# The last quarter of Q by seven-product runs, reciprocals stored on the ACT queue, and a later second weight block

## The chip, the cores and the metric

The kernel runs on one core of one Trainium2 chip. The metric is the device time of one execution in microseconds; smaller is better. The program has five instruction streams that meet only at semaphores: PE (TensorE), DVE (VectorE), ACT (ScalarE), POOL (GpSimd) and SP (SyncE, which here only issues transfers).

## The reference

One transformer block on 2048 tokens (S) of width 1024 (D): a linear attention with 32 heads of 32, and then an MLP that mixes the tokens.

```
x = A_x;  phi = lambda t: where(t > 0, t + 1, exp(t)) + 1e-6
q, k, v = split(layernorm(x) @ wqkv)            # 1024 x 3072
kv  = einsum("bhsd,bhse->bhde", phi(k), v);  z = sum_s phi(k)
num = einsum("bhqd,bhde->bhqe", phi(q), kv)
den = einsum("bhqd,bhd->bhq", phi(q), z)[..., None] + 1e-6
h   = x + (num / den) @ wo
out = h + (gelu(layernorm(h)^T @ w1 + b1) @ w2 + b2)^T    # w1: 2048 x 3584
```

## The kernel before

The work is done in four stages, one after the other.

**Projection stage.** x is normalized and transposed (`xnT`). K and V are made for pairs of token blocks q = 1 to 7 by "runs": a run computes a product of 2 x 2 blocks with seven multiplications instead of eight (Winograd's scheme), p1 to p7, each of four 512-column matmuls. The sums of blocks that it needs are made by DVE (`x_sums`, `w_sums`). `run_step` (L1117) lays two runs over each other: it starts run n and finishes run `prev`, and puts each copy and sum between the matmuls by hand.

Q is kept transposed as `pqT`, eight blocks j of 128 rows for each quarter u of the tokens (512 tokens each), after phi. There are two ways to make it. `q_unit` (and `q_held`, the same with its place in the order fixed) makes one block (u, j) by eight 512-column matmuls; its phi takes an exp and a relu on ACT and two operations on DVE. `QRun` (L1084) makes half a quarter (four j) by the seven products, each of eight 256-column matmuls; before, this is used for quarter u = 2 alone, with two runs laid among the K and V runs of q = 5. The other quarters, u = 0, 1 and 3, are plain units, listed in `q_units` (L1308): eight of them (u = 0) fill places in the projection stage, sixteen (u = 1 and u = 3) come after it.

`kv_accum(i)` adds token block i to kv and z in three PSUM banks; after the last block DVE moves them to `kvbd` and `zz`.

**Fold loop** (L1571). Each turn n makes one remaining Q unit with `q_held`. In turns 1 to 8 it also calls `fold(n - 1)`, two matmuls that multiply kv into wo; ACT copies one result out and DVE the other. PSUM tiles come from a ring of five (`acc_tile`). For each quarter the loop further does:

- `den(u)`: eight matmuls of phi(q) with z (`den_mm`), then on ACT a Ln and an Exp that leave the reciprocal in the one buffer `rd_sb`, and a transfer of it to DRAM (`den_inv`);
- `den_spread(u)`: eight transfers that read it back, repeated over 32 partitions each, into two of three SBUF buffers (`thirds`);
- `scale_q(u, h)`: one DVE multiplication of half a quarter of `pqT`, 128 x 2048 elements.

`den_at`, `spread_at` and `scale_at` give the turns in which they stand. `first_sums` makes sums of the first block of w1 on DVE in the turns of `sums_at`: four `asums` (128 x 2048 each) and four small ones.

**Output stage** (L1598). For each of 16 token blocks i, `seed` lets ACT copy x into two PSUM tiles, `out_mm` adds 16 matmuls of `pqT` with the folded wo, and `out_evac` copies the result to h (ACT) and takes its statistics (DVE). `normalize_h` and `combine_h` prepare the MLP's operand on DVE. Block i reads quarter i // 4 of `pqT`; within one tile the first four matmuls read the half h = 0 and the last four h = 1.

**MLP stages.** Two stages of nested seven-product schemes follow. They are the longer half of the time and the change does not touch their code.

Nearly all instructions of the fold loop and the output stage go through wrappers (`hv`, `ht`, `hs`, `hd` for DVE, PE, ACT and SP) that keep the written order, so that an engine does its instructions strictly as the Python code lists them; they all show line L234, that of the wrapper. Transfers go out on SP's queue in the written order too, and one that waits holds up all behind it.

## Time and profile before

| what | value |
|---|---|
| median of 5 runs | 559.14 us (558.59 to 559.59) |
| the profiled execution: its own time | 559.14 us |
| its span in the profile | 557.3 us |
| granted TensorE clock | 1.0 |
| projection stage, until the last `kv_accum` ends | to 137.4 us |
| fold loop, with the transposes of kv | 142.6 to 176.9 us |
| output stage | 176.9 to 232.8 us |
| PE, DVE, ACT busy, of the span | 99%, 80%, 52% |

A busy PE in this profile only says that matmuls were in flight. What tells whether PE loses time is the distance from the start of one group of matmuls to the start of the next, and whether the next group starts late.

### The profile page before, as it was taken

Reading aid. Unit: us, or ns where it says so; the run is one execution under the profiler, and the core shown is the slowest. Engines: PE = TensorE matmul, PEld = TensorE weight load, DVE = VectorE, ACT = ScalarE, POOL = GpSimd, SP = SyncE. Lnnn points to the kernel's source line nnn. Section 1 sums busy time; section 2 is a strip of 40 time slices with the busy share of each in tenths; the row PEclk is TensorE's granted clock in tenths of the full one; section 3 lists DMA queues with packets and bytes.
Section 4 is the critical chain, followed back from the end, with each engine's and each line's share of the span. In section 5 each row is a group of like instructions: output and inputs, shape, how many; then the busy total and the mean of one; then the engine's idle time right before and its main releaser. Section 6 shows DMA issues by size and latency. Waiting matters only on the chain.

```text
span 557.3 us, 8932 instructions
## 1 busy us (share of the span) xinstructions
PE 551.7 (99%) x3387; PEld 320.4 (57%) x3387; DVE 443.9 (80%) x858; ACT 288.9 (52%) x614; POOL 26.2 (5%) x36
## 2 busy tenths in 40 slices
PE   8999999999999999999999999999999999999997
PEld 3444446645444444456666766666444667667665
DVE  6898888764488688889989789887996879749747
ACT  5747678665776877646556465464210412413311
POOL 1000000000000000000000000000003103103111
PEclk9999999999999999999999999999999999999999
DMA  8933341202966961102140440413769649849434
GB/s 299 306 76 76 84 88 20 39 0 76 313 159 183 331 187 75 76 0 94 60 152 7 145 138 16 151 42 92 204 204 237 195 131 247 208 130 233 94 106 75
DMA packets 83931, 74.51 MB, mean 134 GB/s; under 512 B 15650, under 2 KB 76336, under 8 KB 83888
## 3 DMA queue, kind: packets, MB, share of 16 engines
q1 hardware_dynamic: 79504, 69.87, 42.2%
q0 software_dynamic: 4096, 3.68, 5.1%
q8 instruction: 26, 0.43, 0.3%
q10 hardware_dynamic: 288, 0.39, 0.2%
q14 instruction: 17, 0.14, 0.1%
HBM read 59.12 MB, written 11.67 MB: 127 GB/s over the span
## 4 chain that ended last, share of the span: by engine, by line
PE 92%; DMA 3%; DVE 2%; ACT 1%; issue 0%; ACTq 0%; DVEq 0%
PE psI L234 23%; PE psC L234 14%; PE acc_t L234 14%; PE psB L234 8%; PE psC L966 4%; PE psB L966 4%; PE psA L966 4%; PE acc_t L888 3%; PE acc_t L1298 2%; PE psB L346 2%; PE psA L346 2%; PE psE L966 2%; PE psC L346 2%; DMA wq<-in_B_w_dram 2%; PE kvps L917 1%; PE psA L234 1%
## 5 line engine op out<-in xcount | busy, mean ns | idle before, releaser
L234 PEld LDWEIGHTS <-is 128*128 128x128 f16 x736 | 71.8, 98 | 31.4 <-DVE is L234 0.5
L234 PEld LDWEIGHTS <-sa 128*128 128x128 f16 x606 | 59.2, 98 | 27.5 <-issue 0.4
L234 PEld LDWEIGHTS <-wq 128*128 128x128 bf16 (+1 forms) x496 | 48.5, 98 | 28.2 <-issue 1.2
L234 PE MATMUL acc_t<-wo_sb,pqT 128*128 128x512 f16 x256 | 55.6, 379 | 0.0
L491 POOL DMA_DIRECT2D out_dram<-wq x28 | 24.3, 927 | 519.3 <-ACT wq L494 487.3
L234 PEld LDWEIGHTS <-pqT 128*128 128x128 bf16 x256 | 25.0, 98 | 30.5 <-issue 0.6
L234 DVE TENSOR_TENSOR t<-psI,t 128x256 f32<-128x256 f32 (+1 forms) x45 | 20.8, 475 | 22.2 <-PE psI L234 20.9
L194 DVE TENSOR_SCALAR e_sb<-e_sb 128x512 bf16<-128x512 bf16 x64 | 18.4, 288 | 21.7 <-ACT e_sb L189 21.5
L234 PE MATMUL psC<-gs,wq 128*128 128x512 f16 x140 | 34.1, 379 | 0.0
L966 PEld LDWEIGHTS <-xs 128*128 128x128 f16 x208 | 20.1, 98 | 22.1 <-DVE xs L955 0.6
L234 PE MATMUL psC<-hT,sa 128*128 128x512 f16 x112 | 31.2, 379 | 0.0
L234 PE MATMUL psI<-hi,is 128*128 128x256 f16 x200 | 30.0, 273 | 0.0
L234 PE MATMUL psB<-hT,sa 128*128 128x512 f16 x112 | 29.7, 379 | 0.0
L234 PE MATMUL acc_t<-xnT,wq_sb 128*128 128x512 bf16 x128 | 29.4, 379 | 0.1
L189 ACT ACTIVATE e_sb<-acc_t 128x512 bf16<-128x512 f32 x32 | 19.1, 598 | 18.6 <-PE acc_t L1298 10.0
L234 DVE BATCH_NORM_STATS2 hst<-acc_t 128x6 f32<-128x512 f32 x32 | 21.4, 692 | 9.1 <-ACT h_bf L234 8.9
L966 PE MATMUL psA<-wkv,xnT 128*128 128x512 bf16 x104 | 26.7, 379 | 0.0
L966 PEld LDWEIGHTS <-xnT 128*128 128x128 bf16 x156 | 15.2, 98 | 18.1 <-issue 0.2
L234 PE MATMUL psC<-hT,wq 128*128 128x512 f16 x96 | 24.6, 379 | 0.0
L234 ACT CAST h_bf<-acc_t 128x512 bf16<-128x512 f32 x32 | 18.4, 582 | 12.0 <-PE acc_t L234 12.0
L234 DVE TENSOR_TENSOR e<-psI,es 128x256 f32<-128x256 f32 x20 | 8.5, 425 | 19.9 <-PE psI L234 19.9
L234 ACT COPY psI<-psI 128x256 f32<-128x256 f32 x50 | 18.0, 360 | 11.6 <-PE psI L234 9.7
(246 smaller groups left out, 1132.7 us busy)
## 6 DMA issues: line engine op xcount, KB each, us to landing
wq<-in_B_w_dram SPq DMA_DIRECT2D x14, 1024.0 KB, 8.0
wq<-in_B_w_dram SPq DMA_DIRECT2D x12, 896.0 KB, 7.4
gs<-parked SPq DMA_DIRECT2D x9, 896.0 KB, 4.7
shared_sb<-rd_dram SPq DMA_DIRECT2D x32, 128.0 KB, 3.8
out_dram<-h_bf SPq DMA_DIRECT2D x16, 256.0 KB, 2.0
x_sb<-in_A_x_dram SPq DMA_DIRECT2D x14, 256.0 KB, 3.0
w2o<-in_B_w_dram SPq DMA_DIRECT2D x4, 896.0 KB, 11.0
out_dram<-wq POOLq DMA_DIRECT2D x28, 128.0 KB, 4.6
```

The source lines that it names most:

```text
L189: pin(nc.scalar.activation(e_sb[:], src, ACT.Exp))
L194: pin(nc.vector.tensor_scalar(e_sb[:], e_sb[:], 1.0, PHI_EPS, ALU.min, ALU.add))
L234: return (lambda *a, **kw: pin(op(*a, **kw))) if self.always or getattr(Held, self.key) else op
L346: pe.matmul(ps[:, cols], lhsT=lhs[:, k, :], rhs=mv(k)[:, cols], start=(start and k == 0), stop=(k == self.nk - 1), skip_group_check=True,)
L491: nc.gpsimd.dma_start(to, ot[:, a:b], accum_op=ALU.add)
L888: mm = nc.tensor.matmul(pp[:, 0:CW], lhsT=xnT[:, kt, i * P:(i + 1) * P], rhs=wkv[:, kt, c * CW:(c + 1) * CW], start=(kt == 0), stop=(kt == ...
L917: pin(nc.tensor.matmul(kv_ps[b][:, sl, :], lhsT=pks[i % NPK][:, j * P:(j + 1) * P], rhs=vaugs[i % NVA][:, j, :], start=False, stop=(i == N ...
L966: pin(nc.tensor.matmul(ps[:], lhsT=lhs[:, k, :], rhs=rhs[:, k, :], start=(start and k == 0), stop=(k == hk2 - 1), skip_group_check=True,))
L1298: nc.tensor.matmul(qp[:, 0:SW], lhsT=wq_sb[:, kt, j * P:(j + 1) * P], rhs=xnT[:, kt, u * SW:(u + 1) * SW], start=(kt == 0), stop=(kt == ND ...
```

## The change

Quarter u = 3 is made by two `QRun`s as well. They come after the K and V runs of q = 7, and the last two `kv_accum` move into the second of them. The operands that the Q runs borrow from `pqT` (`later`) lie in other places of it. Of the plain units thirteen are left where there were twenty-one: one beside the end of the last run, and twelve in the fold loop (u = 0, blocks 4 to 7, and u = 1).

In the fold loop the order of the quarters changes: the reciprocals come in the order 2, 0, 3, and 1, whose heads are done in two halves, the second one in the output stage, between the two tiles of block 0. For the halves the unused rows of `zz` are set to S by two small memsets in turn 7. The store of each reciprocal goes out on ACT's queue instead of SP's. The first weight block and the x blocks are loaded later (turns 0 and 6), the second weight block at blocks 8 and 9 of the output stage instead of turns 12 and 13. One `asums` moves to block 10 of the output stage, as does one `scale_q` to block 0 and one to block 2. `TURN` rotates the ring of PSUM tiles once.

```diff
--- before.py
+++ after.py
@@ -819,7 +819,7 @@
                 t.bitcast(FP16).rearrange("p (k c) -> p k c", c=CW)
                 for t in (wo_sb[:, 2 * t:2 * t + 2, :].rearrange("p a b -> p (a b)") for t in range(4))
             ]
-            later = [pqT[:, j:j + 4, u * SW:(u + 1) * SW].bitcast(FP16) for u, j in ((1, 0), (NSC - 1, 0), (NSC - 1, 4))]
+            later = [pqT[:, j:j + 4, u * SW:(u + 1) * SW].bitcast(FP16) for u, j in ((1, 0), (1, 4), (0, 4))]
             tk = [t.bitcast(FP16).rearrange("p (k c) -> p k c", c=CW) for t in thirds] + [later[0]]
             tq = [
                 t.bitcast(FP16).rearrange("p (k j f) -> p k j f", k=ND // 2, f=P)
@@ -1305,7 +1305,7 @@
                 phi_evac(pqT[:, j, u * SW:(u + 1) * SW], qp[:, 0:SW], SW, a2k)
 
             assert NSC == 4
-            q_units = [(u, j) for u in (0, 1, NSC - 1) for j in range(ND)]
+            q_units = [(u, j) for u in range(2) for j in range(ND)]
             NVP = NS // 2
             q_next = iter(q_units)
 
@@ -1338,6 +1338,8 @@
                 runs = [KRun(q), VRun(q)]
                 if q == 5:
                     runs = [runs[0], QRun(q // 2, 0), runs[1], QRun(q // 2, 1)]
+                elif q == NVP - 1:
+                    runs += [QRun(q // 2, 0), QRun(q // 2, 1)]
                 for n in runs:
                     kind = type(n).__name__[0]
                     i = {"K": 2 * q + 3, "V": 2 * q + 4}.get(kind, NS)
@@ -1354,6 +1356,9 @@
                         if kind == "V":
                             kv_accum(2 * q - 2)
                             kv_accum(2 * q - 1)
+                        if kind == "Q" and q == NVP - 1 and n.half == 1:
+                            kv_accum(NS - 2)
+                            kv_accum(NS - 1)
                         if i < NS:
                             ln_finish(i)
                             load_next(i + 2)
@@ -1361,7 +1366,7 @@
                     def after7():
                         if kind == "V" and q != 5 and q + 1 < NVP:
                             x_sums(q + 1)
-                        if kind == "Q" and n.half == 1:
+                        if kind == "Q" and n.half == 1 and q + 1 < NVP:
                             x_sums(q + 1, slice(0, 3))
                         if kind == "K" and q in q_sums:
                             w_sums(qmov, q_sums[q])
@@ -1373,11 +1378,7 @@
                     run_step(n, prev, after6, after5, after7, after3=after3)
                     prev = n
             run_step(None, prev, fill=q_fill)
-            q_fill()
-            kv_accum(NS - 2)
-            kv_accum(NS - 1)
-            for n in range(3):
-                q_fill()
+            q_left = list(q_next)
             nc.vector.memset(zz[:, :, 0:3 * HB], 0.0)
             nc.vector.memset(zz[:, :, 3 * HB:], float(S))
             for b in range(NKB):
@@ -1408,6 +1409,7 @@
         pools["is_bufs"] = 4
         a3p = actx.enter_context(ExitStack())
         ndp = a3p.enter_context(tc.tile_pool(name="ndp", bufs=3, space=PSUM))
+        rd_half = dram.tile([P, SW], FP16, name="rd_half")
         rd_dram = [dram.tile([P, SW], FP16, name=f"rd_dram{u}") for u in range(NSC)]
 
         with ExitStack() as a3:
@@ -1428,33 +1430,34 @@
                     (hs.copy if c == 0 else hv.tensor_copy)(wf[:, j, cols], ps[:, 0:CW])
 
             rdbs = {}
-            SPREAD = (0, 2, 1, 3)
+            SPREAD = (2, 0, 1, 3)
+            TURN = 9
             NH = ND // 2
 
-            def den_mm(u):
+            def den_mm(u, os=(0, 1)):
                 ps = ndp.tile([P, SW], F32, tag="den", name="den_ps")
-                for o in range(2):
+                for o in os:
                     for g in range(4):
                         j = 4 * o + g
                         ht.matmul(
                             ps[g * QR:(g + 1) * QR, :],
                             lhsT=zz[:, j, (1 - o) * HB:(1 - o) * HB + QR],
                             rhs=pqT[:, j, u * SW:(u + 1) * SW],
-                            start=(o == 0),
-                            stop=(o == 1),
+                            start=(o == os[0]),
+                            stop=(o == os[-1]),
                             skip_group_check=True,
                             tile_position=(0, g * QR),
                         )
                 return ps
 
-            def den_inv(u, ps):
+            def den_inv(ps, to):
                 hs.activation(ps[:], ps[:], ACT.Ln, bias=eps_den[:], scale=1.0 / S)
                 hs.activation(rd_sb, ps[:], ACT.Exp, scale=-1.0)
-                hd.dma_start(rd_dram[u][:], rd_sb)
-
-            def den_spread(u):
-                rows = rd_dram[u].rearrange("(g o h) n -> o h g n", g=4, h=HB)
-                for h in range(2):
+                hs.dma_start(to[:], rd_sb)
+
+            def den_spread(u, halves=(0, 1)):
+                for h in halves:
+                    rows = (rd_half if (u, h) == (1, 0) else rd_dram[u]).rearrange("(g o h) n -> o h g n", g=4, h=HB)
                     rdb = thirds[(2 * SPREAD.index(u) + h) % 3].bitcast(FP16).rearrange("p (j n) -> p j n", n=SW)
                     for q in range(HB):
                         hd.dma_start(
@@ -1463,8 +1466,8 @@
                         )
                     rdbs[u, h] = rdb
 
-            def den(u):
-                den_inv(u, den_mm(u))
+            def den(u, os=(0, 1)):
+                den_inv(den_mm(u, os), rd_half if os == (0,) else rd_dram[u])
 
             def scale_q(u, h):
                 v = pqT[:, h * NH:(h + 1) * NH, u * SW:(u + 1) * SW]
@@ -1504,11 +1507,11 @@
 
             def place(i):
                 u, r = divmod(i, NSC)
-                return i if u != 2 else NSC * u + r % 2 * 2 + r // 2
-
-            def out_mm(i):
+                return i if u < 2 else NSC * u + r % 2 * 2 + r // 2
+
+            def out_mm(i, dcs=range(NDC)):
                 at = place(i) * P
-                for dc in range(NDC):
+                for dc in dcs:
                     for j in range(ND):
                         ht.matmul(
                             seeds[i][dc][:, 0:CW],
@@ -1546,44 +1549,52 @@
 
             for c in range(NDC):
                 load_wo(c)
-            for half in range(2):
-                load_w1(0, half, pin)
-            for i in range(XRL + 1):
-                load_xr(i)
-
             def first_sums():
                 cur = Quad([Mixer1(0), Mixer1(1)])
-                for m in (5, 6, 7, 3):
+                for m in (5, 6, 7):
                     yield pin(cur.asums(m))
                 cur.in5 = Inner(cur.sts, 5, None, "i5", cur.sink5, cur.sum5)
                 Held.on = True
                 cur.in5.sums()
                 Held.on = False
                 yield cur
+                pin(cur.asums(3))
+                yield
 
             for _ in range(2):
                 acc_ring.append(acc_ring.pop(0))
-            sums_at, ahead = (4, 8, 9, 11, 13), first_sums()
-            scale_at = {5: (0, 0), 6: (0, 1), 10: (2, 0), 12: (2, 1), 15: (1, 0)}
-            den_at = {0: 0, 2: 2, 9: 1}
-            spread_at = {0: 0, 6: 2, 12: 1}
-            kv_transpose()
-            for n, (u, j) in enumerate(q_units[8:]):
-                if n == len(q_units) - 8 - 1:
+            sums_at, ahead = (4, 5, 8, 11), first_sums()
+            scale_at = {6: (2, 0), 7: (2, 1), 9: (0, 0), 10: (0, 1)}
+            den_at = {1: 2, 4: 0, 6: NSC - 1, 8: 1}
+            spread_at = {3: 2, 6: 0, 10: 1}
+            for n, (u, j) in enumerate(q_left):
+                if n == len(q_left) - 1:
                     seed(0)
                 q_held(u, j)
+                if n == 0:
+                    kv_transpose()
+                    for half in range(2):
+                        load_w1(0, half, pin)
+                    load_xr(0)
                 if 1 <= n < 1 + ND:
                     fold(n - 1)
+                if n == 7:
+                    for at in (0, 2 * HB):
+                        hv.memset(zz[:, :, at:at + HB], float(S))
                 if n in den_at:
-                    den(den_at[n])
-                if n in spread_at:
-                    den_spread(spread_at[n])
-                if n in (12, 13):
-                    load_w1(1, n % 2, pin)
+                    den(den_at[n], (0,) if den_at[n] == 1 else (0, 1))
                 if n in scale_at:
                     scale_q(*scale_at[n])
+                if n in spread_at:
+                    den_spread(spread_at[n], (0,) if spread_at[n] == 1 else (0, 1))
+                    if n == 6:
+                        for i in range(1, XRL + 1):
+                            load_xr(i)
                 if n in sums_at:
                     cur = next(ahead)
+                if n == TURN:
+                    for _ in range(4):
+                        acc_ring.append(acc_ring.pop(0))
             xctx.close()
             a3w = a3.enter_context(tc.tile_pool(name="a3w", bufs=4))
             xr2pool = a3.enter_context(tc.tile_pool(name="xr2pool", bufs=XR2))
@@ -1594,17 +1605,26 @@
             hT2 = hpool.tile([P, NSP, CW], FP16, name="hT2")
             hT3 = hpool.tile([P, NSP, CW], FP16, name="hT3")
             hT4 = hpool.tile([P, NSP, CW], FP16, name="hT4")
-            scale_at = {0: (1, 1), 6: (3, 0), 8: (3, 1)}
+            scale_at = {0: (1, 0), 2: (1, 1), 6: (3, 0), 8: (3, 1)}
             for i in range(NS):
                 seed(i + 1)
-                out_mm(i)
                 if i == 0:
                     load_xr(XRL + 1)
-                    den(NSC - 1)
-                    for k in range(XRL + 2, XRL + XR2 + 1):
+                    out_mm(0, (0,))
+                    den(1, (1,))
+                    load_xr(XRL + 2)
+                    den_spread(1, (1,))
+                    out_mm(0, (1,))
+                    for k in range(XRL + 3, XRL + XR2 + 1):
                         load_xr(k)
-                if i == 2:
+                else:
+                    out_mm(i)
+                if i == 4:
                     den_spread(NSC - 1)
+                if i in (8, 9):
+                    load_w1(1, i % 2, pin)
+                if i == 10:
+                    next(ahead)
                 if i < NS - XRL - XR2 - 1:
                     load_xr(i + XRL + XR2 + 1)
                 if i == NS - 1:
```

## The prediction

> **What bounds the kernel now.** I read the page's engine lines first, then busy time by stretch, then the order of time on PE, DVE, ACT and SP around the fold loop.
>
> ```profile
> PE 551.7 (99%) x3387; PEld 320.4 (57%) x3387; DVE 443.9 (80%) x858; ACT 288.9 (52%) x614; POOL 26.2 (5%) x36
> ```
>
> A stretch's numbers are its length, then PE, PEld, DVE, ACT and POOL busy (instructions), the clock, the DMA share and GB/s:
>
> ```profile
> 143.00:157.00 14.00, 13.60 (x76) 5.54 (x74) 6.26 (x16) 11.23 (x21) 0.00 (x0) 1.00 0.77 253
> 157.00:177.00 20.00, 20.00 (x99) 8.78 (x98) 19.02 (x36) 14.58 (x28) 0.00 (x0) 1.00 0.61 146
> 176.88:232.79 55.91, 55.91 (x266) 25.08 (x265) 45.35 (x94) 40.59 (x96) 0.00 (x0) 1.00 0.57 186
> ```
>
> PE sets the time everywhere, at a clock of 1.00. But in the second half of the fold loop (157 to 177) DVE is busy 19.02 of 20.00 us: it works just behind PE.
>
> ```profile
> 102.58 1.04 PE L1103 MATMUL psA<-xnT,wq_sb 128*128 128x256 bf16 x8
> 103.45 1.04 PE L1103 MATMUL psE<-xs,shared_sb 128*128 128x256 f16 x8
> 131.28 1.89 PE L1298 MATMUL acc_t<-xnT,wq_sb 128*128 128x512 bf16 x8
> 133.00 1.03 PE L966 MATMUL psB<-wkv,xs 128*128 128x512 bf16 x4
> 154.26 0.38 PE L234 MATMUL acc_t<-wo_sb,kvT 128*128 128x512 bf16 x1
> 154.94 0.38 PE L234 MATMUL acc_t<-wo_sb,kvT 128*128 128x512 bf16 x1 [0.30 <-ACT r_sb L191]
> 155.42 1.89 PE L234 MATMUL acc_t<-xnT,wq_sb 128*128 128x512 bf16 x8
> ```
>
> Starts count here. A plain unit takes 1.727 us (24 matmuls in 5.18), a 256-column product 0.874 (three in 2.62), a 512-column matmul 0.216. From 154.26 to 155.42 two matmuls take 1.16 us instead of 0.43: PE lost 0.72. ACT tells why:
>
> ```profile
> 153.31 0.60 ACT L234 ACTIVATE shared_sb<-den_ps 128x512 f16<-128x512 f32 x1 [1.69 <-DMA rd_dram<-shared_sb]
> ```
>
> and the chain of waits, which shows that store:
>
> ```profile
> 147.25 5.98 DMA rd_dram<-shared_sb
> ```
>
> The Exp of the second reciprocal waited for the one buffer's first store, 5.98 us long, and all ACT copies of PSUM waited behind it. Last, DVE's spacing in the loop:
>
> ```profile
> 169.06 0.29 DVE L194 TENSOR_SCALAR e_sb<-e_sb 128x512 bf16<-128x512 bf16 x1
> 169.47 0.42 DVE L198 TENSOR_TENSOR pqT<-e_sb,r_sb 128x512 bf16<-128x512 bf16 x1
> 169.81 1.22 DVE L234 TENSOR_TENSOR pqT<-pqT,shared_sb 128x2048 bf16<-128x2048 bf16 x1
> 170.95 0.29 DVE L194 TENSOR_SCALAR e_sb<-e_sb 128x512 bf16<-128x512 bf16 x1
> ```
>
> From start to start: phi's two operations 0.39 + 0.34 = 0.73, a scaling 1.14 (an `asums` the same), and by the rows at 165.46 and 166.06 a fold copy 0.60.
>
> **The change, part by part.** The profiled execution took 559.14 us, which is also the median of the runs (its span is 557.3, the 1.8 around it are not touched); the sum is made against it.
>
> *Quarter 3 by runs.* Eight units less, 8 x 1.727 = 13.82 us; fourteen products more, 14 x 0.874 = 12.23. All of it is PE's path: -1.58. Their seven products bring per run three copies on ACT and two additions on DVE, in 6.1 us of PE; the Q runs among K and V at 86 to 112 carried more than that with no late start. The last `kv_accum` would end at 143.6; DVE then needs about 3.3 us for `kvbd`, `zz` and a run's addition, until 147, and the transposes are due at 149.66, after turn 0 (147.93 to 149.66). Covered. If it were not, each us late would cost one.
>
> By the Trainium skill (TensorE: Matmul & The Clock Gate, Back-to-back issue gap) a sustained stream has 81 ns per matmul at 128 columns and 131 at 512; a straight line between gives my estimate of 98 ns at 256, so the exchange would lose 112 x 98 - 64 x 131 = 2.6 us. The rows above show 216 and 109 ns here, and I go by them.
>
> *The stall at 154.26.* New stores are three turns, then two apart. The first is issued at 155.2 and the next Exp is due at 161.5: 6.3 us, over the 5.98. The weight block, which now waits until the last run's DVE work is done (151.0), is mostly through by then. -0.72. If the store took longer, ACT and all evacuations behind it would wait again; 1.69 us of that cost PE 0.72. What is late next is below.
>
> *Store on ACT's queue.* An issue takes 0.41 us of ACT by the row at 0.74 us (`x_sb`, ACTq), against 0.34 on SP. Per folding turn ACT works 1.46 of 2.16 us (exp 0.50, relu 0.48, copy 0.48), and a reciprocal adds 1.4 + 0.41: the lag is made up in the next turns. Nothing on the path by itself. Its landing lies, by the rows, between 1.7 us (one in light traffic) and 5.98; I take 2 to 4. By the Trainium skill (DMA: Bandwidth & Descriptors, Issuing engines are not separate DMA queues) the transfers of all queues interleave on the same 16 engines, so the other queue would not help the store against a weight block; by it the store keeps its 5.98 and the sum stays as it is.
>
> *Halving quarter 1's heads.* The same eight matmuls in two groups; a group begins 0.09 late (starts at 144.76 due, 144.85 seen): +0.09. The second Ln, Exp and store are ACT time in the output stage, where ACT is busy 40.59 of 55.91.
>
> *kv to fold.* Between the transposes and the first fold there is now one unit instead of two units and the heads. ACT needs 2.2 us from the end of a unit to the end of `kvT` (142.58 to 144.77), PE gets there 2.18 after it and needs about 0.1 more to restart: +0.15, bounds 0 and 0.5.
>
> *DVE in the shorter loop.* This decides. Turns end on PE (no stalls after the first fold) at 161.92 (n = 5), 164.08, 166.88, 169.04, 171.56, 173.29 and 175.02 (n = 11). Turn 5's phi starts its addition on DVE at 163.63, because ACT first does quarter 0's Ln, Exp and store. From there DVE has, in its fixed order: the addition, copy and `asums` (2.07), turn 6 with a scaling (2.47), turn 7 with a scaling, a short wait and the two memsets of about 0.08 each (2.69), turn 8 with `asums` (2.46), turns 9 and 10 with a scaling each (1.87 + 1.87). 13.43 in all: the last scaling, half 1 of quarter 0, ends at 177.06. `out_mm(0)` starts at 175.12 and its fifth matmul, at 175.98, reads that half: it starts at about 177.2. +1.22. The first half heads on the way wait for the memsets (end 169.72, due 169.5), a stall of 0.3 that lies within the 1.22. Before, quarter 0 was scaled eight turns before its use. Bounds: 0.4, if DVE starts its chain at turn 5's relu without the Ln and Exp before it (about 0.8 earlier); 2.0, if the weight block (issued 151.0; such loads took 5.4 to 11.0 to land) holds the first `asums`, due at 161.4, by 0.8.
>
> *Reads and x blocks.* On SP everything is queued in order: quarter 2's eight reads (from about 158), quarter 0's (the second half only after the scaling that frees its buffer at 168.2 and quarter 3's store, about 169.4), x blocks 1 to 3, then quarter 1's first half, two x blocks, its second half, six x blocks. Eight reads take about 3.6 us to issue and 3.9 to land. Quarter 0's would land at about 174.7, needed at 175.9; quarter 1's second half is stored at 180.4, read from 182.6, landed at about 188, and DVE comes to it at 188.7; PE needs it scaled at 191.4, so 190.2 would do. Covered by 1 to 2 us. x blocks come at least two blocks early.
>
> *Moved to the output stage.* One more scaling, four small sums and an `asums`: 3.7 us more DVE work on 45.35 of 55.91, spread to blocks 0, 2 and 10, where DVE idles about 1.15 per pair of blocks; it has caught up before block 15. The second weight block is issued at about 208, lands by 219 (11.0 at most), and its first use was at 246.9. Nothing.
>
> Sum: -1.58 - 0.72 + 0.09 + 0.15 + 1.22 = -0.84; 559.14 becomes 558.3. Nothing after the output stage changes its order, so the gain is carried to the end.
>
> **The rivals.** *DVE's cover holds.* If the chain on DVE ends a us earlier, only PE's terms remain: -1.58 - 0.72 + 0.09 + 0.15 = -2.06, 557.1. For it: the old loop ran 20 us at 95% DVE without a late matmul. Against it: there the last scaling before the output stage was not read at once.
>
> *A round trip of reciprocals comes late* (the slower side). In the old output stage the eight reads of quarter 3 took longer:
>
> ```profile
> 189.01 5.17 SPq L234 DMA_DIRECT2D shared_sb<-rd_dram  x8
> ```
>
> 5.17 us to issue, and with 5.0 to land (median of that stretch) about 10 us from first issue to last landing. If quarter 1's second half takes 10 us from 182.6, it lands at 192.6 instead of by 190.2. Block 4 waits 2.4 us: -0.84 + 2.4 = +1.6, 560.7. It decides from a landing at 190.2 on. Against it: then x blocks and a weight block filled the engines; now the x blocks are queued behind the reads, and there are four reads, not eight.
>
> **How the numbers follow.** A measurement of this kernel can tell about 0.2%, 1.1 us, from no change: the lines are 558.0 and 560.3. The forecast gets 0.50, with a range of its own from 557.3 to 559.4 (the stall from 0.4 to 2.0 and the `kvT` term from 0 to 0.5); 0.18 of it lies under 558.0. DVE's cover holds: 0.28. A late round trip: 0.22, of which 0.18 lies above 560.3. So faster 0.28 + 0.18 = 0.46, slower 0.18, the same 0.36. The range goes from 557.0 to 560.2; it leaves out most of the late round trip and a little below.
>
> **What would show it.** In the changed profile: fourteen more products at 0.874; no ACT wait of over a us on `rd_dram`; the first fold about 0.15 late; the first half heads waiting for a memset; and the fifth matmul of `out_mm(0)` about a us after the fourth, released by DVE's scaling. If `out_mm(0)` runs its sixteen matmuls in 3.5 us, the DVE chain was mis-sized. If block 4 starts late or DVE waits for a transfer in the output stage, the rival on the slower side holds. Wrong altogether: a late start in the projection stage after 131, or a change in the MLP stages.

## The result, and the profile after

The changed kernel takes 560.84 us (median of 33 runs, 558.72 to 563.14) where the kernel before took 559.09 in the same session (57 runs, 557.97 to 560.13). The ratio is 1.0027, with a 95% interval from 1.002 to 1.0035. A gain of 0.8 us was forecast, a loss of 1.75 came, and the new kernel's times are spread twice as wide. Its profiled execution took 561.92 us (span 560.1), one of its slower ones, so its rows show more than the median loss.

From its page, the engines and the chain that ended last (the chain by engine was PE 92%, DMA 3%, DVE 2% before):

```profile
PE 550.3 (98%) x3435; PEld 324.9 (58%) x3435; DVE 447.4 (80%) x864; ACT 291.4 (52%) x618; POOL 26.3 (5%) x36
...
PE 84%; DMA 8%; DVE 5%; ACT 2%; issue 1%; SPq 0%; ACTq 0%; DVEq 0%
```

PE was busy 1.4 us less and finished 2.8 us later: the matmuls saved are real, and transfers (8% of the chain) took the place of matmuls. Busy time by stretch (length, then PE, PEld, DVE, ACT, POOL, clock, DMA share, GB/s) says where; these are the second half of the fold loop and the output stage.

```profile
157.00:175.45 18.45, 18.24 (x98) 7.47 (x96) 15.79 (x30) 15.59 (x30) 0.00 (x0) 1.00 0.66 200
175.45:233.14 57.69, 56.02 (x261) 24.97 (x260) 48.37 (x98) 40.80 (x96) 0.00 (x0) 1.00 0.67 210
```

The output stage was 55.91 us of unbroken PE; now it is 57.69 with 56.02 busy. The starts on PE show each place (a number in brackets is the idle time before the row, and what ended it):

```profile
131.35 1.04 PE L1103 MATMUL psA<-xnT,wq_sb 128*128 128x256 bf16 x8
...
169.83 0.40 PE L234 MATMUL den_ps<-pqT,zz 128*32 128x512 bf16 x4 [0.21 <-DVE zz L234]
...
175.45 1.02 PE L234 MATMUL acc_t<-wo_sb,pqT 128*128 128x512 f16 x4
177.50 1.04 PE L234 MATMUL acc_t<-wo_sb,pqT 128*128 128x512 f16 x4 [1.03 <-DVE pqT L234]
...
198.61 34.69 PE L234 MATMUL acc_t<-wo_sb,pqT 128*128 128x512 f16 x160 [0.65 <-ACT acc_t L234]
...
474.32 0.94 PE L234 MATMUL psI<-gi,is 128*128 128x256 f16 x7 [0.94 <-DVE is L234]
```

Up to the output stage nearly all is as forecast: `out_mm(0)` starts at 175.45 instead of 176.88 (175.12 was forecast), and its fifth matmul waits for DVE. The waits at 198.61 and 474.32 were not forecast. The first is a wait for ACT, which waits for a store, and behind that stands the order of SP's queue:

```profile
196.58 1.07 ACT L234 CAST h_bf<-acc_t 128x512 bf16<-128x512 f32 x2 [3.47 <-DMA out_dram<-h_bf]
```

```profile
160.71 11.84 SPq L234 DMA_DIRECT2D shared_sb<-rd_dram  x16
172.59 3.71 SPq L234 DMA_DIRECT2D shared_sb<-in_A_x_dram  x3
...
183.96 1.75 SPq L234 DMA_DIRECT2D shared_sb<-rd_dram  x4
185.75 2.81 SPq L234 DMA_DIRECT2D xr<-in_A_x_dram  x6
...
189.73 0.34 SPq L234 DMA_DIRECT2D out_dram<-h_bf  x1
```

h has four buffers (`h_bf`). Block 0's h was ready by 181.7, but its store stands on SP behind the reads of quarter 1's second half, which wait until 183.96 for the landing of that half's reciprocals, and behind seven x blocks; it leaves at 189.73, lands at 196.50 and only then frees its buffer for block 4. Before, it left earlier, landed at 192.46, and nothing waited:

```profile
187.02 0.34 SPq L234 DMA_DIRECT2D out_dram<-h_bf  x1
```

The wait at 474.32 is DVE's, for a weight block of the second MLP stage:

```profile
472.98 0.62 DVE L234 TENSOR_TENSOR is<-wq 128x896 f16<-128x896 bf16 x1 [1.46 <-DMA wq<-in_B_w_dram]
```

Before, this operation began without a wait:

```profile
471.10 0.61 DVE L234 TENSOR_TENSOR is<-wq 128x896 f16<-128x896 bf16 x1
```

The `load_w2` calls stand at the same place against PE in both kernels (4.5 us ahead of the same matmul), yet the second block of the pair took 10.3 us to land instead of 8.0. The same happens once more at the next pair, with a wait of 0.91 us on PE at 515.33. At the end the kernel is 2.78 us behind: 0.07 from before 131, 0.28 from there to the end of the output stage, 2.43 from the MLP stages.

### The profile page after: what moved, and what is told of

The parts are those of the page before. It is cut to its first block, busy times and chain, and to the rows that moved or that the text cites. A ratio compares the mean times of both kernels' runs of the same rounds, so it can differ in the third digit from the quotient of the medians.

```text
span 560.1 us, 9040 instructions
## 1 busy us (share of the span) xinstructions
PE 550.3 (98%) x3435; PEld 324.9 (58%) x3435; DVE 447.4 (80%) x864; ACT 291.4 (52%) x618; POOL 26.3 (5%) x36
## 4 chain that ended last, share of the span: by engine, by line
PE 84%; DMA 8%; DVE 5%; ACT 2%; issue 1%; SPq 0%; ACTq 0%; DVEq 0%
PE psI L234 21%; PE psC L234 13%; PE acc_t L234 8%; PE psB L234 8%; PE psC L966 4%; PE psB L966 4%; PE psA L966 4%; DMA wq<-in_B_w_dram 4%; PE acc_t L888 3%; PE psB L346 2%; PE psA L346 2%; PE psE L966 2%; PE psC L346 2%; DVE is L234 1%; DMA shared_sb<-rd_dram 1%; PE kvps L917 1%
## 5 line engine op out<-in xcount | busy, mean ns | idle before, releaser
L234 PE MATMUL psI<-gi,is 128*128 128x256 f16 x168 | 22.3, 273 | 1.8 <-DVE is L234 1.8
L234 PE MATMUL acc_t<-xnT,wq_sb 128*128 128x512 bf16 x96 | 22.4, 379 | 0.0
## 6 DMA issues: line engine op xcount, KB each, us to landing
w2o<-in_B_w_dram SPq DMA_DIRECT2D x4, 896.0 KB, 10.3
```

The costliest lines, as they stand in the source:

```text
L234: return (lambda *a, **kw: pin(op(*a, **kw))) if self.always or getattr(Held, self.key) else op
```

## The experiments

The stages of every profiled execution, cut at starts on PE (second last pair of `kv_accum`, first matmul of `out_mm(0)`, first of each MLP stage, last matmul; the first MLP stage is 159.64 to 159.68 in all and left out). The last two columns are the first and second pair of w2 loads of the second MLP stage: when the load's last packet starts, counted from the load's issue, and in brackets when a packet of the instruction queue q8 starts amid them, less than 10 us after the issue. Times in us; the last is the profiled execution's own.

```
                                to kv   loop  output  MLP 2   w2, first     w2, second     own
before                         129.47  47.41  55.90  161.40   9.92         11.11 (8.79)  559.14
after                          129.55  45.90  57.70  163.85  12.05 (0.90)  12.06         561.92
e1 after, shared tile          129.40  46.52  58.19  163.41  13.17 (0.81)  10.00         562.37
e2 before, DRAM shifted        129.86  47.31  55.90  162.26  10.39         12.01 (9.13)  560.31
e3 before, half w2             130.54  47.35  55.90  160.86   6.88          6.62 (8.88)  559.64
e4 after, half w2              130.81  46.06  58.43  160.86   8.07 (5.73)   6.66         561.00
e5 after, x loads later        129.95  46.06  56.83  160.86   9.94 (1.02)  10.15         558.53
e6 + half rows first           130.84  46.10  57.67  162.99  12.77 (0.72)  10.32         562.46
e7 after, stores on SP         129.69  47.10  57.38  162.17  11.25 (1.58)  11.23         561.18
e8 before, stores on ACT       129.83  47.56  56.00  160.96  10.11         10.69 (8.79)  559.30
e9 before, 48 more on PE       131.18  46.98  55.90  161.78  11.51 (0.59)  10.17         560.77
e10 after, 34 more on PE       130.22  45.83  58.67  160.86   9.72         10.40         560.41
e11 e6, 34 more on PE          130.91  45.84  58.51  160.86   9.86         10.33         560.95
e12 e5, other block order      130.63  46.04  56.72  161.83  11.54 (0.65)  10.25         560.06
e13 e12, 18 more on PE         129.92  45.86  56.76  160.91  10.12         10.64         558.29
e14 after, 18 more on PE       130.54  45.86  57.35  160.86   9.99          9.98         559.46
e15 e8 again                   129.93  47.80  57.11  161.45   9.81         11.17 (9.39)  561.25
e16 e13, quarter 0 later       130.40  45.85  55.83  160.86   9.96         10.36         557.86
e17 e16, stores on POOL        131.13  45.62  55.83  162.65  10.39         12.45         560.44
e18 after, stores on POOL      129.34  45.63  57.93  160.86  10.51 (0.71)   9.94         558.93
```

The first column varies by 1.8 us whatever the kernel, so a single execution's own time settles little; the stages settle more. Each ratio below is against the kernel before on the same chip.

**Where do the late weights come from? The place in DRAM (e1, e2).** The change adds a DRAM tile, `rd_half`, which moves the parked tiles of the MLP.

```diff
 e1 (after)
-        rd_half = dram.tile([P, SW], FP16, name="rd_half")
+        rd_half = rd_dram[1]          # set behind rd_dram
 e2 (before)
+        rd_dram = [dram.tile([(1 + u // 3) * P, SW], FP16, name=f"rd_dram{u}")[0:P, :] for u in range(NSC)]
```

> The changed kernel, but the first half's reciprocals of quarter 1 are stored into quarter 1's own DRAM tile, so that there is no extra DRAM tile of 128 KB and the parked tiles of the second MLP stage lie where they lay before the change (606208 instead of 737280). Nothing else moves. Theory P (place: the extra tile shifts what the second MLP stage reads and makes its w2 loads land later): the two waits for w2 (1.46 us on the vector engine at 472.98, the like at 513.99) go, about 2.4 us less: 558.5 to 559.3, close to the kernel before. Rival Q (place does not matter; it comes from the transfers on the ACT queue or from the run): still 560.3 to 561.3. The stalls at out_mm(0) (1.03 us) and at h_bf (3.47 us on ACT) stay in both.

> The kernel before, with one of its four reciprocal tiles in DRAM made twice as long (the second half unused), so that the parked tiles lie 131072 bytes higher, as they do in the changed kernel. No instruction is changed. Theory P: the w2 loads of the second MLP stage land about 1 to 2 us later and the kernel comes out at 560.5 to 561.5. Rival Q: 558.8 to 559.5, as the kernel before.

e1: 562.37, 1.0048 (1.0026 to 1.007); its first w2 pair is late all the same. e2: 559.03, 1.001 (0.9998 to 1.0023). The place is not the cause. (e1 also makes quarter 1's second store wait for the reads of the first: it leaves at 183.46 instead of 180.27, and PE waits 0.39 us more, at 185.45.)

**How much do the weights cost? Half of w2 (e3, e4).** `load_w2` in `next2` loads `slice(0, NFP // 2)` of the rows; the kernel leaves out half of these weights.

> The kernel before, with the first-half w2 loads of the later pairs (two DMAs of 896 KB for each pair of mixers) cut to half of the rows; the other half of the tile keeps old data, so this leaves out half of those weights. It takes the second MLP stage's loads off the path. Theory W (what the change lost beyond the output stage is lost in waits for these loads): the wait at 512.5 goes here, 0.5 to 1.5 us under the kernel before (557.6 to 558.6), and this kernel and its changed twin differ by 0.3 to 0.5 us. Rival (the loss is spread over the MLP stages): this one as the kernel before, 559.1, its twin 1.5 to 2 us slower.

> The changed kernel with the same w2 loads cut to half of the rows (half of those weights left out). Theory W: 558.0 to 559.0, 0.3 to 0.5 us over the same cut of the kernel before, which is what the trace shows at the end of the output stage. Rival: 559.5 to 560.8, 1.5 to 2 us over its twin.

558.74, 1.000 (0.9991 to 1.001), and 559.57, 1.0012 (0.9997 to 1.0026). The second MLP stage is 160.86 in both: with light loads the kernels are equal there. Neither theory has the times. Before itself lost 0.54 to the loads in its profile, yet e3's median is no better than before's. The twins differ by 0.83 instead of the 0.3 to 0.5 of theory W or the 1.5 to 2 of its rival: the w2 loads would make about half of the loss of 1.75, with wide intervals. In e4's profile, one of its slower runs, the output stage lost 2.5 us and not the 1.8 of the first one. That stage, too, varies from run to run.

**The output stage: x loads later (e5), and half the rows first (e6).**

```diff
 e5: in block 0
-                    for k in range(XRL + 3, XRL + XR2 + 1):
-                        load_xr(k)
                 out_evac(i)
+                if i == 0:
+                    for k in range(XRL + 3, XRL + XR2 + 1):
+                        load_xr(k)
 e6, besides
-                    out_mm(0, (0,))           # one column half, all eight j
+                    out_mm(0, range(NH))      # both column halves, j = 0 to 3
```

> The changed kernel, but the six loads of x that the SP queue carries in block 0 of the output stage are put behind block 0's own store (out_dram<-h_bf). Theory S (the store of block 0 leaves late, at 189.73, behind these six loads and the reads of the reciprocals, and block 4's copy to h_bf waits for it): the store leaves at about 186 and lands before block 4 needs its buffer at 193.1; ACT's wait of 3.47 us at 196.58 and PE's 0.65 us at 198.61 go, the output stage is 0.6 to 1.2 us shorter than the changed kernel's 57.69 us. Rival (the store is slow on the memory side, whenever it leaves): it still lands at 196 and the stage stays at 57.7 or more. Neither touches the w2 waits behind.

> As the last one, and block 0's sixteen matmuls run the first four head groups of both column halves before the last four of both, with the second half of the reciprocals of quarter 1 between: four more matmuls (0.87 us) lie ahead of the one that waits for the last scaling of quarter 0. Theory D (the 1.03 us at 177.50 is a plain wait for that scaling, which ends at 177.06): the wait falls to 0.0 to 0.4 us, and the output stage to 55.9 to 56.5 us, against 55.91 in the kernel before; the kernel is then 0.7 to 1.5 us faster than before in every run in which w2 is not late (557.3 to 558.1), and near 559 if w2 stays late. Rival (the vector engine is the bound there and gives the time back later): the output stage stays above 57 us.

e5: 559.50, 1.0016 (1.0002 to 1.003). SP's and PE's rows of e5:

```profile
186.75 0.38 SPq L234 DMA_DIRECT2D out_dram<-h_bf  x1
```

```profile
178.00 1.04 PE L234 MATMUL acc_t<-wo_sb,pqT 128*128 128x512 f16 x4 [0.97 <-DVE pqT L234]
178.97 0.40 PE L234 MATMUL den_ps<-pqT,zz 128*32 128x512 bf16 x4
179.30 53.70 PE L234 MATMUL acc_t<-wo_sb,pqT 128*128 128x512 f16 x248
```

The store leaves 3 us earlier, the stage is 0.87 us shorter, and all blocks behind run without a break: theory S holds. e6: 559.35, 1.0006 (0.9993 to 1.0018), with its output stage at 57.67 where theory D had at most 56.5. The wait moved: the last of the second half's four head matmuls now waits 1.62 us, at 180.77, for the last Q unit's phi, which stands on DVE behind the scaling of quarter 0, which in this run waited 1.32 us for its reads. So the wait at `out_mm(0)` is not DVE's work alone, it is the reads' landing too.

**The queue of the stores (e7, e8, e15).** `hs.dma_start(to[:], rd_sb)` becomes `hd...` in e7; the reverse edit in the kernel before gives e8, and e15 is e8 run and profiled once more.

> The changed kernel with the stores of the reciprocals on the SP queue again. Theory A (the second queue changes how the later transfers of SP are served, which is why w2 lands late): the w2 waits go, 2.4 us less in the second MLP stage; what the queue order costs in the fold loop is 0 to 2 us. Rival N (w2's lateness has nothing to do with that queue): the second MLP stage stays at 162.5 to 164 us against 161.40 before, and the kernel is the same as the changed one or up to 2 us slower, since stores and reads of SP wait in line.

> The kernel before with nothing changed but the queue of the reciprocals' four stores: ACT instead of SP. Theory A: w2 lands late here too, the second MLP stage at 162.5 to 164 us instead of 161.40, and the kernel at 560 to 561.5. Rival N: the second MLP stage as before; the fold loop 0 to 0.7 us shorter (the wait of the Exp at 153 for its buffer shrinks) plus 4 x 0.33 us of issue on ACT that lies in its idle time; 558.2 to 559.1.

> A second look at the kernel before with the reciprocals' stores on the ACT queue, whose median was 1.2 us above before while its one profiled run was among its fastest and showed 0.25 us of it. Theory G (the loss lies in waits that differ from run to run): one of the stages shows a wait of 0.5 to 2 us that the first look did not have. Rival: nothing but the time in which the first loads land differs.

e7: 562.00, 1.0061 (1.0037 to 1.0084), with its loop 1.2 us longer than after's. Without ACT's queue the new loop is worse, and w2 still lands late (11.25 and 11.23), which speaks against theory A. e8: 560.28, 1.0027 (1.0015 to 1.004): on ACT's queue the old kernel is worse as well. Theory A had this time but a late w2 as its cause, and the second MLP stage is 160.96; rival N had the cause right and the time too low. The first profile of this kernel loses 0.25 us in the loop and the output stage, the second (e15, 561.25, a single execution) 1.6, most of it in the output stage. ACT's row and SP's rows of e15:

```profile
205.17 1.07 ACT L234 CAST h_bf<-acc_t 128x512 bf16<-128x512 f32 x2 [2.59 <-DMA out_dram<-h_bf]
```

```profile
188.78 2.24 SPq L234 DMA_DIRECT2D xr<-in_A_x_dram  x5
...
191.59 0.38 SPq L234 DMA_DIRECT2D out_dram<-h_bf  x1
```

It is the wait for `h_bf` again: these x loads left from 183.84 on in the kernel before and leave from 188.78 on here, when the reciprocal that ACT stored at 183.34 has landed (188.76), though they have nothing to do with it; the stores of h follow behind them. The trace gives the reason: in these programs the transfers on SP and ACT take eight completion semaphores (100, 102, 111, 112, 114, 115, 116, 118) in turn, and each waits until the transfer eight before it has landed. That ACT store and the x load at 188.78 both carry 118. So a store on ACT's queue still holds SP, eight transfers later.

**TensorE's instruction packets (e9, e10, e11, e14).** In the packets of the trace, a late w2 load ends in packets that start one by one, mostly 0.12 us apart. Its completion semaphore, which counts to 16, says the same: for the second load of after's first pair 15 of the 16 steps have come by 10.3 us after the pair's issue, and the last comes at 12.6. One of 16 shares is behind the others. The page's third part has a queue q8 with 27 packets of 16 KB for the 6870 instructions of PE and PEld, one for some 256; each takes about 1 us. The queues while the first pair of w2 loads was under way, in after (460.4 to 470.4):

```profile
q1 hardware_dynamic: 3651, 2.12, 75.8%
q0 software_dynamic: 362, 0.33, 21.4%
q8 instruction: 1, 0.02, 0.6%
```

In the same stretch of before (460.1 to 470.0) the q8 row is missing; there the packet started at 470.2. The change adds 48 matmuls ahead of the MLP and so moves the packets. In e9 the kernel before gets 48 more in its warm-up (e13 and the later e16 and e17 have the warm-up of e14):

```diff
             mm(warm[:, 0:min(w, P)], warm[:, 0:w])
...
-            warm_up(6)
+            warm_up(54, w=48)     # e9; e10 and e11: 40; e14 and e13: 20, then warm_up(4) as before
```

> The kernel before with 48 more matmuls on TensorE in its warm-up: 54 of 48 columns in place of six of 512, on the same zero tile, ahead of the first data. Nothing else is changed; the kernel then has as many TensorE instructions ahead of the MLP stages as the changed one. In the trace of before, a 16 KB packet of the instruction queue q8 (974 ns) starts 10.13 us after the first w2 load of the second MLP stage was issued, when the load's packets have all started (the last at 9.94); in the changed kernel it starts at 0.90, amid them, and the load's last packets trickle out at 0.12 us apart until 11.42. Theory F (the change moves TensorE's instruction fetches, one for some 256 instructions, into the w2 loads): here the packet starts 1 to 4 us after the load's issue, the last w2 packets start at 10.5 to 11.5, PE waits 0.5 to 2 us at its first matmuls on that load, and the median is 0.5 to 1.5 us over the kernel before. Rival R (lateness of the load is chance, or comes from the ACT queue): no wait there, and 558.6 to 559.4.

> The changed kernel with 34 more matmuls in the warm-up (40 of 48 columns in place of six of 512). By the spacing of the q8 packets in its trace (461.3, 478.8, 497.4, 517.6) 68 more instructions move them some 5 us earlier, to about 456, 474, 492 and 512.5: between the w2 loads, not into them. Theory F: no wait for w2 at 472 to 474, the second MLP stage 160.9 to 161.9 us instead of 163.85; the stalls of the output stage stay; median 559.0 to 560.0. Rival R: the stage stays at 162.5 to 164 and the median at 560.5 to 561.

> The kernel with the six loads of x behind block 0's store and the first head groups first in block 0, with the same 34 more matmuls in the warm-up. Theory F: the late w2 goes here too, so that the upper half of its spread (559.3 to 562.5) thins out; median 557.8 to 558.6, under the kernel before. Rival R: as without them, near 559.3 with the same spread.

> The changed kernel with the same 18 more matmuls in the warm-up and nothing else. Theory F: the second MLP stage 160.9 to 161.6 us; the output stage keeps its 57.7 us or more; median 559.2 to 560.2, 0.6 to 1.6 us under the changed kernel. Rival: the stage 162.5 to 164, median 560.5 to 561.

The packets went about where they were expected (table), and in these four runs the late load came and went with them. In e9 DVE waits where after's did, and PE for 0.35 us behind it:

```profile
473.33 0.62 DVE L234 TENSOR_TENSOR is<-wq 128x896 f16<-128x896 bf16 x1 [0.88 <-DMA wq<-in_B_w_dram]
```

In e10, e11 and e14 the stage is 160.86. Over the 36 pairs of whole w2 loads in the table, the last packet started later than 10.9 us in 9 of 12 with a q8 packet amid them, in 3 of 14 with a packet of q14 alone (the other instruction queue, 8 KB), and in none of 10 without either (e2's first pair, with a packet at 10.15, and e17's second, at 11.04, count as not met). So theory F holds for a good part of the late loads, not for all. After's own second pair met no q8 packet, only one of q14 8.4 us after its issue, and is as late as the first, again with one share behind: 15 of 16 steps by 10.5 us, the last at 12.6. Of the 2.99 us that after's stage is over the undisturbed 160.86 of e10, e11 and e14, 1.51 arise at the first pair and 1.48 at the second. In e5 and e18 a packet amid the first pair did no harm. By the Trainium skill (DMA: Bandwidth & Descriptors, Queues, rings and completion order) a DMA is split over up to 16 engines, and an engine changes between queues only at packet boundaries; by its section on why a DMA increments its semaphore by 16 and not by 1, only the full 16 means that all data has landed. That fits a single engine left behind by a packet, but the trace does not say which engine a packet ran on, and a packet of 1 us alone does not explain a load that is 1 to 3 us late: why stays open.

What it is worth in the time is less sure. e9 came to 560.71, 1.0026 (1.0015 to 1.0038), but of the 1.63 us that its profile lost 1.71 lies in the first stage and only 0.38 in the second MLP stage (0.92 at the first pair, less the 0.54 that before loses at the second, which was no longer hit). e10 came to 560.25, 1.0028 (1.0014 to 1.0042), e14 to 559.93, 1.0031 (1.0015 to 1.0048): the stage shrank as expected, but the times do not differ from after's 1.0027, where theory F had e14 0.6 to 1.6 us under it. The altered warm-up is a rival here: the first stage is 130.77 on average in e9 to e11 and 130.50 in e13, e14, e16 and e17, against 129.99 in the thirteen other profiles (129.34 to 130.84). Whether the warm-up costs that was not tried. In e10 and e11 (561.45, 1.0043, 1.0028 to 1.0059, far over the 558.6 that was expected at most) the output stage grew to 58.5 to 58.7; PE's rows of e10:

```profile
178.70 1.04 PE L234 MATMUL acc_t<-wo_sb,pqT 128*128 128x512 f16 x4 [1.62 <-DVE pqT L234]
...
194.14 6.22 PE L234 MATMUL acc_t<-wo_sb,pqT 128*128 128x512 f16 x28 [1.01 <-DVE pqT L234]
```

At 194.14 block 4 waits for quarter 1's second half: the prediction's late round trip, real in these two runs, where its reads left at 186.8 and 187.5 instead of 183.96. The shifted q8 packets now start at 184.6 and 185.2, amid that round trip; whether they cause it was not tried.

**The order of the blocks (e12, e13, e16).** The output stage begins with quarter 2, whose scaling is done by 171; x, the output, `pqT` and `hE`/`hO` are indexed by `blk(i)`. All three have e5's x loads.

```diff
+            def blk(i):
+                return i + 8 if i < 4 else i - 4 if i < 12 else i
 e16, besides
-            scale_at = {6: (2, 0), 7: (2, 1), 9: (0, 0), 10: (0, 1)}
+            scale_at = {6: (2, 0), 7: (2, 1), 10: (0, 0)}
...
-            scale_at = {0: (1, 0), 2: (1, 1), 6: (3, 0), 8: (3, 1)}
+            scale_at = {0: (0, 1), 2: (1, 0), 4: (1, 1), 6: (3, 0), 8: (3, 1)}
```

> The changed kernel with the six loads of x behind block 0's store, and with the output stage's blocks in another order: those of quarter 2 first, then quarters 0, 1 and 3. Quarter 2 is scaled by 171, four microseconds ahead of the stage; quarter 0 is then wanted at about 190 and quarter 1 at 204. Theory O (what the output stage loses is the round trips of the reciprocals, wanted too early): no wait in the stage, 55.9 to 56.3 us as in the kernel before; 1.3 to 1.6 us under before at the stage's end. The w2 loads still meet the instruction packet: median 558.4 to 559.5, some runs below 558. Rival (the vector engine is full there): the waits move to later blocks, the stage stays over 57 us, the median over 559.5.

> As the last one, with 18 more matmuls in the warm-up (20 of 48 columns and four of 512 in place of six of 512, which takes as long). 36 instructions move the q8 packets of the changed kernel some 2.6 us earlier: 458.7 and 494.8, ahead of the w2 loads. Theories O and F together: the output stage 55.9 to 56.3, the second MLP stage 160.9 to 161.6, median 557.3 to 558.3, faster than the kernel before by 0.8 to 1.5 us. If F is wrong: as the last one.

> As e13 (blocks of quarter 2 first, x loads behind block 0's store, 18 more matmuls in the warm-up), and the second half of quarter 0 is scaled in block 0 of the output stage instead of in turn 10 of the loop; quarter 1's scalings follow at blocks 2 and 4. Theory O: the 0.83 to 0.87 us that e12 and e13 still lose ahead of the second half's denominators (TensorE waits for the last Q evacuations, which stand on the vector engine behind a scaling that waits for its reads) go; the output stage 55.9 to 56.1 us, the median 557.6 to 558.4, 0.3 to 1.0 under the kernel before. Rival: another wait takes its place and the median stays at 558.8 or more.

e12: 559.70, 1.0019 (1.0009 to 1.0028); e13: 559.09, 1.0009 (0.9997 to 1.002): both over the times expected, and e12, the new order on top of e5's edit, is no better than e5. The block waits are gone, and one that costs 0.8 us is left, the one that e6 had uncovered. DVE's and PE's rows of e12:

```profile
177.53 1.23 DVE L234 TENSOR_TENSOR pqT<-pqT,shared_sb 128x2048 bf16<-128x2048 bf16 x1 [0.36 <-DMA shared_sb<-rd_dram]
```

```profile
179.54 0.38 PE L234 MATMUL den_ps<-pqT,zz 128*32 128x512 bf16 x1 [0.66 <-DVE pqT L198]
```

e16 moves that scaling behind the last phi. It takes 557.86, 0.9979 (0.997 to 0.9988): faster than the kernel before by 1.2 us, as expected, with all eleven runs between 557.40 and 558.41. PE's rows of e16:

```profile
176.24 1.89 PE L234 MATMUL acc_t<-wo_sb,pqT 128*128 128x512 f16 x8
178.06 0.55 PE L234 MATMUL den_ps<-pqT,zz 128*32 128x512 bf16 x4
178.54 53.70 PE L234 MATMUL acc_t<-wo_sb,pqT 128*128 128x512 f16 x248
232.07 3.62 PE L234 MATMUL psA<-hE,wq 128*128 128x512 f16 x16
```

The output stage is 55.83 us with no wait, and the loop keeps its 1.5 us. With the deadlines eased, the spread is gone too (1.0 us), with the stores still on ACT's queue. Of the 1.28 us by which e16's profiled execution beats before's, the loop and the output stage make 1.63 and the second MLP stage 0.54, while the first stage is 0.93 longer. The kernel before with its packets moved out of the w2 loads was not tried, so how much of e16's gain the moved packets make is open.

**Stores on GpSimd's queue (e17, e18).** `hg.dma_start(to[:], rd_sb)` with `hg` the wrapper of GpSimd, in e16 and in the changed kernel.

> As e16, with the reciprocals' stores on GpSimd's queue instead of ACT's. Transfers of the ACT and SP queues share eight completion semaphores in turn, so that a load on SP waits for a store on ACT eight transfers ahead; those of GpSimd have semaphores of their own. Theory L (that sharing is what holds SP and makes the spread between runs): SP is not held for the stores of quarters 3 and 1, and the spread of the times shrinks to that of the kernel before (1.7 us); median 557.2 to 558.2. Rival: GpSimd's store lands later by 1 us or more and the reads with it; as e16 or up to 1 us slower.

> The changed kernel with the reciprocals' stores on GpSimd's queue and nothing else. Theory L: in the changed kernel SP's reads for the second half of quarter 0 leave at 170.81, when quarter 3's store has landed, though the data they wait for was free at 168.3; here they leave at about 168.4, the scaling on the vector engine no longer waits for them (0.27 to 1.32 us), and the x load of 175.47 leaves by 173. The wait at out_mm(0) falls by 0.2 to 1.2 us. The second half of quarter 1 comes 0.5 to 1.5 us later by GpSimd's issue, so that block 4 may wait for it: median 559.5 to 561. Rival: the reads leave at 170.5 or later as before, and the wait at out_mm(0) stays over 1 us.

SP's and PE's rows of e18:

```profile
160.50 10.14 SPq L234 DMA_DIRECT2D shared_sb<-rd_dram  x16
170.69 1.38 SPq L234 DMA_DIRECT2D shared_sb<-in_A_x_dram  x3
```

```profile
176.66 1.04 PE L234 MATMUL acc_t<-wo_sb,pqT 128*128 128x512 f16 x4 [0.67 <-DVE pqT L234]
...
198.37 34.69 PE L234 MATMUL acc_t<-wo_sb,pqT 128*128 128x512 f16 x160 [1.08 <-ACT acc_t L234]
```

GpSimd's stores use other semaphores (105 to 109). The reads of quarter 0's second half leave at 168.75 instead of 170.81 (in the changed kernel they carry 112, which quarter 3's store had until 170.32), the x loads follow without a gap, DVE's scaling waits for no transfer, and the wait at `out_mm(0)` is 0.67 instead of 1.03. So sharing semaphores is what held SP, and about 0.7 is the part of the wait that is DVE's own (ACT, which feeds DVE, no longer issues the stores here). The kernel is no faster for it, 559.99, 1.0026 (1.0012 to 1.004); in the profile block 4 still waits for `h_bf`. e17 came to 558.67, 0.9989 (0.9978 to 1.0001), no better than e16; its profiled run lost 1.8 us to a late w2, at a pair with no q8 packet in its first 10 us. The spread did not shrink (3.0 us in e17, 3.6 in e18): the semaphores do not explain it.

## Why the prediction was wrong, point by point

The matmuls saved were forecast right. What failed is the step "Reads and x blocks", which put the transfers of the output stage at nothing and cost about 1.2 us, and behind it the sentence that the gain is carried to the end, which cost about 0.8 us. A slip in the sum adds 0.3.

- **Quarter 3 by runs: right.** Fourteen products at 0.874 us, no late start, the last two `kv_accum` from 142.69 to 143.6.
- **The stall at 154.26: right.** It is gone; the store took 5.8 us (issued 154.87, read from 160.71) and nothing waited for it.
- **kvT to fold: right, 0.07 late instead of 0.15.** The halved heads wait for the memset as forecast, 0.37 us behind their due start against 0.3.
- **The sum itself: 0.3 too good.** The stall of the half heads was taken as lying within the 1.22, but the prediction's own clock times (fifth matmul at 177.2, before 177.74) gave a gain of 0.54. Measured: 177.50, less 0.07 from the first stage, so 0.31.
- **DVE in the shorter loop: the place right, part of the cause missed.** The fifth matmul waits 1.03 us in after (1.19 late from start to start, where 1.22 was forecast) and 1.62 in e10. That the size fits is in part luck: DVE alone makes about 0.7 of the wait (e18). The rest is the step "Reads and x blocks": quarter 0's second half was to land at 174.7, because quarter 3's store would have landed at 169.4. It landed at 170.3, 3.2 us after its issue, the reads left at 170.81 and landed by 176.1, and DVE, due to start that scaling at 175.95, waited 0.27 us (1.32 in e6).
- **"x blocks come at least two blocks early" counted the wrong transfers: this is where the step failed.** What stands behind quarter 1's reads on SP is not only x but the stores of h, and those give back the buffers for block 4. The prediction lists SP's queue in order and never lists `out_dram<-h_bf`. PE waited for it 0.65 to 1.2 us at 198.4 to 200.8 in after, e4 and e18, and hardly in e7 and e14.
- **The late round trip: seldom, but real.** In after the second half lands at 189.66, DVE waits 0.58 us for it and scales it just in time; in e10 and e11 it is 3 us later and block 4 waits 1.0 and 1.55 us. That this rival's 560.7 lies next to the measured 560.84 is luck: it had all of the loss in that one wait, and PE does not wait for it in after.
- **"Nothing after the output stage changes its order, so the gain is carried to the end": wrong, though the order did not change.** The prediction itself named a change in the MLP stages as a sign of being wrong altogether. What moved was TensorE's instruction packets, which explains part of it. The seven profiles with the changed loop and a packet in the first pair (after, e1, e5, e6, e7, e12, e18) have a second MLP stage of 162.28 us on average, the kernels before (before, e2, e8, e15) 161.52: some 0.8 us, between groups that scatter by 3.0 and 1.3.

The four profiles with the unrepaired loop and output stage (after, e4, e10, e14) gain 1.50 us in the loop on average and lose 2.14 in the output stage, of which DVE's own stall makes some 0.8 to 0.9 from start to start and the transfers the other 1.2 to 1.3; with the 0.8 that is a loss of 1.4, of the 1.75 measured. The rest is within the scatter of the first stage. That e14's repair of the late load did not show in its time leaves the size of the 0.8 open. That e16, with all repairs, is 1.2 us faster than before speaks for the saved matmuls, though the moved packets may have a part in it.

## What to carry to other kernels

Before moving a transfer, list every transfer behind it on its queue and what each gives back: here the harmless-looking one was a store that frees a buffer four blocks later. A stage that ran just ahead of its transfers turns each us saved into a deadline. No single repair made this kernel faster than the one before (e5 1.0016, e6 1.0006, e14 1.0031, e18 1.0026); together they did (e16 0.9979): when several waits lie close behind each other, taking one away uncovers the next. And code that is not touched can slow down when instructions are added ahead of it (e9), so compare the stages of several profiles before looking for the cause inside the change.

## What the hardware showed that was not expected

- TensorE's instructions come in 16 KB packets on q8, one for some 256 instructions, about 1 us each. A weight load of 2 x 896 KB that met one ended late in 9 of 12 cases, by 1 to 3 us, its last packets mostly 0.12 us apart; without one it ended late in 3 of 24.
- A store on ACT's queue held loads on SP for 2.1 us (reads at 170.81 against 168.75 in e18) and 5 us (x loads at 188.78 against 183.84 in the kernel before), through the completion semaphores that both queues use in turn; stores on GpSimd's queue did not.
- The landing of one 128 KB store took 3.2 to 5.8 us in the changed kernel, and a 256 KB store 6.8 us, with other transfers under way.
